# Moving the operands of one matmul family by 192 bytes: longer tiles of probabilities and of r in an attention and feed-forward kernel

## The chip, the cores and the metric

The kernel runs on one core of a Trainium2 chip. The metric is the device time of one execution in microseconds (us); the number that stands for a kernel is the median of several executions. A core has a matrix engine (TensorE: PE for its matmuls, PEld for the loads of its stationary operand), VectorE (DVE), ScalarE (ACT), GpSimd (POOL), and SyncE (SP), which here issues the DMAs. SBUF is the working memory, with 128 partitions; an address below is a byte address within a partition. PSUM is the memory that matmuls write.

## The reference

Windowed attention with block summaries, and behind it a feed-forward layer with a squared ReLU. Cut to what matters:

```python
k_sum = k.reshape(B, H, nb, 32, D).max(axis=3)         # B, H, S, D = 4, 8, 768, 64
v_sum = v.reshape(B, H, nb, 32, D).mean(axis=3)
scores_l = where(|i - j| < 16, q @ k.T / 8, -1e9)
scores_s = q @ k_sum.T / 8 + log(32)
a = softmax(concat([scores_l, scores_s]))
x = (a @ concat([v, v_sum])).reshape(3072, 512)        # heads side by side
h = x @ w_in                                           # 512 x 2048
g = s * maximum(h, 0)**2 + b
return g @ w_out                                       # 2048 x 512
```

## The kernel before

The 3072 tokens are worked in 12 chunks of 256 (`c`). A chunk has three parts on PE. The attention of its 8 heads (lines 274 to 417) ends in the attended values. The hidden layer, `hidden` (line 460), makes for each of 16 blocks of 128 hidden units (`f`) one 128x256 result in PSUM. The projection, `project` (line 504), adds each block's contribution to two 128x512 outputs.

Both matrix products of the feed-forward layer are done at fp32 accuracy with the one-pass type F32R, by splitting each operand into an upper and a lower part and adding three products: lower times upper, upper times lower, upper times upper. The attended values of a chunk are split into `xh` and `xl` (128 partitions, 4 blocks of 256 values, 4096 bytes a partition, two buffers each, so that one chunk's can be written while the other's are read). The weights are split into `wh` and `wl`. The activated values `g` are split into halves `gh` and `gl` (512 values, 2048 bytes, four buffers each).

The operand that is loaded into the array and stays there is the stationary one; the operand that is streamed past it is the moving one. In `hidden` the moving operand is a block of 256 values of `xh` or `xl`, and the stationary one 128 columns of `wl` or `wh`. In `project` it is the other way about: 512 columns of `wh` or `wl` move, and 128 columns of `gh` or `gl` are stationary. Every matmul of the two has its own load, so PE runs through pairs of a load and a matmul: 12 pairs for one `f` of `hidden`, 6 for one of `project`.

From chunk 2 on a planner sets the order: steps are numbered by hidden block; `hidden` is called for four blocks in a row (48 pairs), then `project` for the four blocks before (24 pairs). Beside these run the attention of a later chunk and the chain that makes `g`: `activate` (relu on ACT into `r`, square in place), `scaled` (POOL, in place), `upper_rows` (`gh`, DVE) and `lower_rows` (`gl`, DVE). The first chunks are written out by hand in `FIRST_ORDER`.

Where a tile lies is set by the pool it comes from. Pools stand one behind the other, and within a pool each name has its buffers one behind the other, in the order in which names are first asked for, each rounded up to 32 bytes. In the pool `p2` the order is `vsum`, `ksum`, `rs`, `pT`, `pr`, `mn`, `sums`, `xh`, `xl`, `r`, `gh`, `gl`, `vhalf`, `vmean`; behind it stands the pool with `qk` and `vw`. `pr` (probabilities of a pair of head pairs, made in `masked`) and `r` (made in `activate`) have two buffers each. In the weights' pools every tile is a multiple of 4096 bytes long, and all `wh` and `wl` start at a multiple of 256. Addresses before, with the remainder by 256:

| tile | first buffer | remainder of its buffers by 256 |
|---|---|---|
| wh (8 tiles), wl (16 tiles) | 4352 and 69888 on | 0 |
| pr | 163264 | 192, 224 |
| mn, sums | 171008, 171136 | 0 to 224 in steps of 32 |
| xh | 171264 | 0, 0 |
| xl | 179456 | 0, 0 |
| r | 187648 | 0, 0 |
| gh | 191744 | 0 in all four |
| gl | 199936 | 0 in all four |
| qk | 208896 | 0, 160, 64, 224 |
| vw | 220800 | 128 in all four |

Of the kernel before, what the change touches and what calls it, by code (L numbers as in the profile page):

```python
# [11 lines left out]
F32 = mybir.dt.float32  # L12
# [7 lines left out]
P = 128  # L20
# [7 lines left out]
KR = WIN + NB  # L28
NSUB = 4
T = NSUB * SUB  # L30
# [14 lines left out]
def windowed_attention_then_relu2_ffn(ctx, tc, qk, vwin, kt, vt, kq, vrow, wp, out):  # L45


    nc = tc.nc
# [5 lines left out]
    p2 = ctx.enter_context(tc.tile_pool(name="p2", bufs=2))  # L54
# [29 lines left out]
    def mask_of(st):  # L84
        return mask_first if st == 0 else mask_last if st == NST - 2 else mask_mid
# [143 lines left out]
    def place(c):  # L229
        return c // PER_B, c % PER_B  # L230
# [75 lines left out]
    def masked(c, p, j):  # L306
        _, ci = place(c)
        if j == 0 and c == 0:
            t = stage.tile([P, 4 * KR + 8], F32, name="pr0", tag="stage")
            pr_of[c, p] = t[:, : 4 * KR].rearrange("p (n k) -> p n k", k=KR)  # L310
            mn_of[c, p], sm_of[c, p] = t[:, 4 * KR : 4 * KR + 4], t[:, 4 * KR + 4 :]
        elif j == 0:
            if (c, p // 2) not in prs_of:
                prs_of[c, p // 2] = p2.tile([P, 8 * KR + 8], F32, name="pr", bufs=2)
                if turns_on_dve(c):
                    nc.gpsimd.memset(prs_of[c, p // 2][:, 8 * KR :], 0.0)
            t = prs_of[c, p // 2][:, 4 * KR * (p % 2) : 4 * KR * (p % 2 + 1)]
            pr_of[c, p] = t.rearrange("p (n k) -> p n k", k=KR)
            mn_of[c, p] = p2.tile([P, 4], F32, name="mn", bufs=4)
            sm_of[c, p] = p2.tile([P, 4], F32, name="sums", bufs=4)  # L320
        for e in range(2):
            n = 2 * e + j
            nc.vector.tensor_tensor_reduce(  # L323
                out=pr_of[c, p][:, n, :], in0=ps_of[c, p][e][:, j, :], in1=mask_of(NSUB * ci + 2 * j),
                scale=-1.0 / math.sqrt(D), scalar=3.0e38, op0=ALU.add, op1=ALU.min,
                accum_out=mn_of[c, p][:, n : n + 1],
            )
        if j == 1:
            ps_of.pop((c, p))
            qk_t.pop((c, p))  # L330
# [17 lines left out]
    prs_of, pTs_of = {}, {}  # L348

    def turns_on_dve(c):  # L350
        return c > 2
# [84 lines left out]
    ph_of, gg, po = {}, {}, {}  # L436
# [25 lines left out]
            )  # L462

    def activate(c, q, other=0):
        gg[c, q] = r = p2.tile([P, 2 * T], F32, name="r")
        ph = ph_of.pop((c, q))
        if other < 2:
            nc.scalar.activation(r, ph, AF.Relu)  # L468
        else:
            nc.vector.tensor_scalar(r, ph, 0.0, None, ALU.max)  # L470
        if other % 2:
            nc.vector.tensor_tensor(r, r, r, ALU.mult)
        else:
            nc.scalar.activation(r, r, AF.Square)  # L474
# [72 lines left out]
    def of(fn, *more):  # L547
# [4 lines left out]
        "i": of(load_weights, "in"), "o": of(load_weights, "out"), "w": of(load_weights, "in", "out"),  # L552
        "u": load_unit, "x": load_values, "L": load_k,
        "W": keep_warm, "K": k_max, "k": fill_k, "Z": scores_of_maxima, "S": scores, "M": masked, "E": exps,
        "N": normalize, "T": transposes, "C": turned, "V": values, "U": values_of_means, "R": mean_of_rows,
        "F": mean_done, "t": fill_v, "X": attended, "y": attended_low, 
        "Ai": of(scale_weights, "in"), "Ao": of(scale_weights, "out"), "A": of(scale_weights, "both"),
        "Bi": of(convert_weights, "in"), "Bo": of(convert_weights, "out"), "D": of(convert_weights, "both"),
        "Y": hidden_part, "H": hidden, "J": activate, "G": scaled, "a": upper_rows, "b": lower_rows,
        "P": project, "O": evict, "h": upper_weights, "l": lower_weights,  # L560
    }
# [20 lines left out]
    for c in range(2, NC):  # L582
        bi, ci = place(c)
        for p in range(NPAIR):
# [15 lines left out]
            for j in range(2):  # L600
                then(base, VISIT, scores, c, p, j)
                then(m, NEXT if p < 2 else ATT, masked, c, p, j)
                then((e0, e1)[j], NEXT if p < 2 else ATT, exps, c, p, j)
# [16 lines left out]
    for i in range(NF, NC * NF):  # L620
        c, f = divmod(i, NF)

        then(i - i % 4, HID, hidden, c, f)
        if f % 2:
            for stage_of in (activate, scaled, upper_rows, lower_rows):
                then(i, CHAIN, stage_of, c, f // 2)
        then((i + 4) | 3, PROJ, project, c, f)
        if f == NF - 1:
            for t in range(T // P):
                then((i + 4) | 3, EVICT, evict, c, t)  # L630
# [60 lines left out]
```

## Time and profile before

| | us |
|---|---|
| median of 3 runs (620.56 to 621.52) | 621.0 |
| the profiled execution's own time | 620.62 |
| its span, first to last instruction | 618.9 |
| granted TensorE clock in it | 0.999 |

The profile is of one execution. A view that groups instructions gives, for a line of the kernel, an engine and an operation, the count, the busy time and the mean or median duration of one. The durations of matmuls overlap, since one starts while the one before is still running out; how often PE starts a matmul is read from start times or from the pieces of the chain. The chain that ended last is followed back from the last instruction to whatever released it, and is PE for nearly its whole length.

### The profile page before, as it was taken

How to read it: one execution, taken by the hardware profiler on the slowest of the kernel's cores; microseconds unless marked ns; L12 is line 12 of the kernel's file. 1: busy time of each engine (PE TensorE's matmuls, PEld its weight loads, DVE VectorE, ACT ScalarE, POOL GpSimd, SP SyncE). 2: the span in 40 equal slices, each digit the busy share in tenths (PEclk: the TensorE clock that was granted, in tenths of full speed). 3: DMA queues.
4: the chain of work that ended last, by engine and by line, in shares of the span. 5: the costliest groups of instructions: out<-in, count | busy, mean ns of one | idle time of the engine just before them, and what ended most of it. 6: DMA issues, size and time to landing. Idle time of an engine off the chain costs nothing.

```text
span 618.9 us, 13522 instructions
## 1 busy us (share of the span) xinstructions
PE 608.4 (98%) x5240; PEld 551.3 (89%) x5240; DVE 418.7 (68%) x1126; ACT 276.6 (45%) x712; POOL 138.0 (22%) x275
## 2 busy tenths in 40 slices
PE   6999999999999999999999999999999999999997
PEld 5798999899889998998999899999998998999896
DVE  6999988689488278568758648947848827832211
ACT  5999997262352362263163154234235235223221
POOL 4420012211410411411131411321141051041110
PEclk9999999999999999999999999999999999999999
DMA  8998722026105017003503112500710500200000
GB/s 338 398 412 325 280 71 109 23 86 195 57 2 182 1 44 255 23 20 103 169 20 128 56 44 72 207 19 28 214 49 1 183 4 16 86 1 1 35 1 34
DMA packets 26993, 66.41 MB, mean 107 GB/s; under 512 B 3824, under 2 KB 3824, under 8 KB 26928
## 3 DMA queue, kind: packets, MB, share of 16 engines
q1 hardware_dynamic: 26928, 65.54, 29.9%
q8 instruction: 41, 0.67, 0.4%
q14 instruction: 24, 0.20, 0.1%
HBM read 59.09 MB, written 6.29 MB: 106 GB/s over the span
## 4 chain that ended last, share of the span: by engine, by line
PE 94%; ACT 3%; POOL 1%; DVE 1%; issue 1%; POOLq 0%; DVEq 0%; ACTq 0%
PE ph L460 44%; PE po L504 43%; PE pav L417 4%; PE ps L301 3%; ACT pr L336 2%; PE pt L379 0%; POOL vw L263 0%; PE ph L441 0%; DVE pr L346 0%; ACT pT L221 0%; ACT wraw L122 0%; ACT wraw L123 0%; POOL mask_first L73 0%; ACT vsum L221 0%; POOL mask_mid L73 0%
## 5 line engine op out<-in xcount | busy, mean ns | idle before, releaser
L481 POOL TENSOR_SCALAR r<-r,sb_col 128x512 f32<-128x512 f32 x85 | 68.9, 811 | 396.2 <-ACT r L474 281.2
L504 PE MATMUL po<-wh,gl 128*128 128x512 f32 x384 | 151.5, 395 | 0.0
L504 PE MATMUL po<-wl,gh 128*128 128x512 f32 x384 | 150.0, 391 | 0.0
L504 PE MATMUL po<-wh,gh 128*128 128x512 f32 x384 | 149.6, 389 | 0.0
L468 ACT ACTIVATE r<-ph 128x512 f32<-128x512 f32 x93 | 55.5, 597 | 209.9 <-PE ph L460 201.8
L219 DVE CAST gh<-r 128x512 fp32r<-128x512 f32 x88 | 38.3, 435 | 143.0 <-POOL r L481 140.3
L368 DVE STREAM_TRANSPOSE pT<-pr 32x256 f32<-32x256 f32 x288 | 125.5, 436 | 4.1
L460 PE MATMUL ph<-xl,wh 128*128 128x256 f32 x760 | 122.2, 283 | 0.0
L460 PE MATMUL ph<-xh,wh 128*128 128x256 f32 x760 | 122.1, 283 | 0.0
L460 PE MATMUL ph<-xh,wl 128*128 128x256 f32 x760 | 122.0, 283 | 0.0
L460 PEld LDWEIGHTS ph<-xh,wl 128*128 128x128 f32 x760 | 108.0, 191 | 4.3 <-issue 0.2
L460 PEld LDWEIGHTS ph<-xh,wh 128*128 128x128 f32 x760 | 104.9, 192 | 0.0
L460 PEld LDWEIGHTS ph<-xl,wh 128*128 128x128 f32 x760 | 104.8, 192 | 0.0
L504 PEld LDWEIGHTS po<-wh,gh 128*128 128x128 f32 x384 | 72.1, 188 | 15.5
L504 PEld LDWEIGHTS po<-wh,gl 128*128 128x128 f32 x384 | 72.3, 188 | 14.9 <-issue 1.0
L504 PEld LDWEIGHTS po<-wl,gh 128*128 128x128 f32 x384 | 72.3, 188 | 12.9
L336 ACT ACTIVATE pr<-pr,mn 128x120 f32<-128x120 f32 x176 | 67.0, 383 | 23.0 <-DVE mn L323 22.8
L492 DVE TENSOR_TENSOR gl<-r,gh 128x512 fp32r<-128x512 f32 x96 | 69.2, 721 | 4.1 <-ACT gh L221 1.3
L474 ACT ACTIVATE r<-r 128x512 f32<-128x512 f32 x92 | 58.1, 632 | 5.4 <-DVE r L470 2.5
L263 POOL COPY vw<-vsum 24x256 f32<-24x256 f32 x88 | 46.7, 565 | 37.1 <-DMA vsum<-vmean 16.4
L221 ACT COPY o<-po 128x512 f32<-128x512 f32 x23 | 13.5, 587 | 45.5 <-PE po L504 44.4
L346 DVE TENSOR_TENSOR pr<-pr,rs 128x480 f32<-128x480 f32 x48 | 32.1, 670 | 2.4 <-ACT pr L336 0.5
(88 smaller groups left out, 480.2 us busy)
## 6 DMA issues: line engine op xcount, KB each, us to landing
wraw<-in_wp_dram SPq DMA_DIRECT2D x32, 512.0 KB
qk<-in_qk_dram SPq DMA_DIRECT2D x44, 369.0 KB
vw<-in_vwin_dram SPq DMA_DIRECT2D x48, 256.0 KB
out_dram<-o SPq DMA_DIRECT2D x24, 256.0 KB
kraw<-in_kt_dram SPq DMA_DIRECT2D x12, 384.0 KB
vraw<-in_vt_dram SPq DMA_DIRECT2D x12, 252.0 KB
kq<-in_kq_dram SPq DMA_DIRECT2D x4, 512.0 KB
vraw<-in_vt_dram SPq DMA_DIRECT2D x6, 264.0 KB
```

Source lines behind the costliest of these rows:

```text
L219: nc.vector.tensor_copy(out_, in_)
L263: nc.gpsimd.tensor_copy(vw_t[c, p][WIN:KR, e], vsum[bi][WIN : WIN + NB, 2 * p + e, :].unsqueeze(1).to_broadcast([NB, NSUB, D]),)
L336: nc.scalar.activation(pr, pr, AF.Exp, bias=mn_of[c, p][:, n : n + 1], scale=-1.0, accum_out=sm_of[c, p][:, n : n + 1])
L346: nc.vector.tensor_tensor(pr, pr, rs.unsqueeze(2).to_broadcast([P, 4, KR]), ALU.mult)
L368: nc.vector.transpose(to[BLOCK * k : BLOCK * (k + 1), :, rows], src)
L417: nc.tensor.matmul(oi, vw[:KR, e, i, :], pi[:KR], start=True, stop=True)
L460: nc.tensor.matmul(ph, w[:, kc * P : (kc + 1) * P], x[:, kc], start=(n == 0), stop=(n == len(terms) - 1))
L468: nc.scalar.activation(r, ph, AF.Relu)
L474: nc.scalar.activation(r, r, AF.Square)
L481: (nc.vector if other else nc.gpsimd).tensor_scalar(g, g, s_col, b_col, ALU.mult, ALU.add)
L492: nc.vector.tensor_tensor(gl, g, gh.bitcast(F32), ALU.subtract)
L504: nc.tensor.matmul(po[c, t], a[:, t * P : (t + 1) * P], w[:, 512:], start=(f == 0 and n == 0), stop=(f == NF - 1 and n == len(terms) - 1),)
```

## The change

Two tiles are asked for at a greater length than is used. `pr` gets 24 more floats (96 bytes) in each of its two buffers, and only the 8 floats that were there are set to zero, as before. `r` gets 8 more floats (32 bytes) in each of its two buffers, and the code goes on with the first 512. No instruction is added, taken away, resized or put elsewhere in the order: on each engine the rows of the two programs are the same.

```diff
-                prs_of[c, p // 2] = p2.tile([P, 8 * KR + 8], F32, name="pr", bufs=2)
+                prs_of[c, p // 2] = p2.tile([P, 8 * KR + 32], F32, name="pr", bufs=2)
                 if turns_on_dve(c):
-                    nc.gpsimd.memset(prs_of[c, p // 2][:, 8 * KR :], 0.0)
+                    nc.gpsimd.memset(prs_of[c, p // 2][:, 8 * KR : 8 * KR + 8], 0.0)
...
-        gg[c, q] = r = p2.tile([P, 2 * T], F32, name="r")
+        gg[c, q] = r = p2.tile([P, 2 * T + 8], F32, name="r")[:, : 2 * T]
```

What moves is addresses. Everything behind `pr` in the pool moves up by 2 x 96 = 192 bytes, and everything behind `r` by 192 + 2 x 32 = 256:

| tile | moved by | remainder by 256 before | after |
|---|---|---|---|
| wh, wl, pT, first buffer of pr | 0 | 0, 0, 192, 192 | the same |
| second buffer of pr | 96 | 224 | 64 |
| mn, sums | 192 | 0 to 224 | 0 to 224 |
| xh, xl (moving operands of `hidden`) | 192 | 0 | 192 |
| r, first and second buffer | 192, 224 | 0, 0 | 192, 224 |
| gh, gl (stationary operands of `project`) | 256 | 0 | 0 |
| qk, vw | 256 | 0, 160, 64, 224 and 128 | the same |

So, by the remainder, the one relation between two operands of a matmul that changes in the feed-forward layer is that of `hidden`: the moving operand starts at 192 where its stationary one starts at 0, where both started at 0.

## The prediction

> **What bounds the kernel now.** I read the page's list of engines first, then the chain that ended last, by line.
>
> ```profile
> span 618.9 us, 13522 instructions
> PE 608.4 (98%) x5240; PEld 551.3 (89%) x5240; DVE 418.7 (68%) x1126; ACT 276.6 (45%) x712; POOL 138.0 (22%) x275
> PE 94%; ACT 3%; POOL 1%; DVE 1%; issue 1%; POOLq 0%; DVEq 0%; ACTq 0%
> ```
>
> PE is busy 98% of the span and the chain lies on it for 94%. A busy PE is not yet a PE at its peak, so the next question is how fast the pairs of load and matmul follow each other. The chain in order of time gives that, because it joins pairs of one line to a piece with a length and a count. Near the end:
>
> ```profile
> 569.92 0.84 PE ph L460 x7
> 570.76 5.47 PE po L504 x24
> 576.22 5.75 PE ph L460 x48
> 581.98 5.47 PE po L504 x24
> 587.44 5.75 PE ph L460 x48
> 593.20 5.47 PE po L504 x24
> 598.66 5.75 PE ph L460 x48
> 604.42 10.92 PE po L504 x48
> ```
>
> Columns: start, length, what, how many. Line 460 (`hidden`) takes 5.75 / 48 = 119.8 ns a pair and 0.84 / 7 = 120 ns within a run; line 504 (`project`) 5.47 / 24 = 227.9 ns. No wait is in between: a piece starts where the last one ended. The kernel's time is therefore mostly two pitches times two counts, and a change of addresses can move it only by moving a pitch, or by turning something beside PE into a wait.
>
> **How much of the pitch is not streaming.** The profile has a family of matmuls that shows what a pair can do, the transposes of line 379.
>
> ```profile
> 108.98 0.82 PE L379 MATMUL pt<-ident,pr 128*120 128x128 f32 x6
> L379 PE MATMUL pt<-ident,pr x48: 270/273/326, 12.6 to 109.7; 128*120 128x128 f32 x48
> ```
>
> Six of them take 0.82 us, the last one's 273 ns included: (820 - 273) / 5 = 109 ns from start to start. Now the two lines of the feed-forward layer, with the least, median and greatest duration of one:
>
> ```profile
> L460 PEld LDWEIGHTS ph<-xh,wl x760: 186/192/192, 36.3 to 603.1; 128*128 128x128 f32 x190
> L460 PE MATMUL ph<-xh,wl x760: 277/283/387, 36.4 to 603.2; 128*128 128x256 f32 x190
> L460 PE MATMUL ph<-xl,wh x760: 280/283/287, 36.9 to 603.7; 128*128 128x256 f32 x190
> L504 PE MATMUL po<-wl,gh x384: 387/389/402, 42.4 to 614.7; 128*128 128x512 f32 x192
> ```
>
> From 256 to 512 columns the median grows by 389 - 283 = 106 ns, so 256 columns stream in about 106 ns. A pair of line 460 thus has 120 - 106 = 14 ns beside its columns, one of line 504 has 227.9 - 212 = 16. But line 460 also has matmuls of 277 ns and loads of 186 where the medians are 283 and 192: something between them costs about 6 ns each, nearly always, and sometimes doesn't.
>
> Where doesn't it? At the switch from `project` to `hidden`. Matmuls from 597.82 us on, start, length and count:
>
> ```profile
> 597.82 0.39 PE L504 MATMUL po<-wh,gl 128*128 128x512 f32 x1
> 598.05 0.39 PE L504 MATMUL po<-wl,gh 128*128 128x512 f32 x1
> 598.27 0.39 PE L504 MATMUL po<-wh,gh 128*128 128x512 f32 x1
> 598.50 0.64 PE L460 MATMUL ph<-xh,wl 128*128 128x256 f32 x4
> 598.97 0.64 PE L460 MATMUL ph<-xl,wh 128*128 128x256 f32 x4
> 599.45 0.28 PE L460 MATMUL ph<-xh,wh 128*128 128x256 f32 x1
> ```
>
> The first four pairs of `hidden` take 0.47 us (598.50 to 598.97), the next four 0.48. The grouped view of the stretch 598.4 to 598.6 has the first alone:
>
> ```profile
> L460 PE MATMUL ph<-xh,wl 128*128 128x256 f32 x1 | 0.3, 278 | 0.0
> ```
>
> It lasts 278 ns, and the pitch behind it is 114 ns; by the third pair it is 120 and stays there. In the other direction the same happens. The first matmuls of `project` after `hidden`:
>
> ```profile
> 593.03 0.40 PE L504 MATMUL po<-wh,gl 128*128 128x512 f32 x1
> 593.27 0.40 PE L504 MATMUL po<-wl,gh 128*128 128x512 f32 x1
> 593.50 0.39 PE L504 MATMUL po<-wh,gh 128*128 128x512 f32 x1
> 593.73 0.40 PE L504 MATMUL po<-wh,gl 128*128 128x512 f32 x1
> 593.96 0.39 PE L504 MATMUL po<-wl,gh 128*128 128x512 f32 x1
> 594.19 0.39 PE L504 MATMUL po<-wh,gh 128*128 128x512 f32 x1
> 594.42 0.39 PE L504 MATMUL po<-wh,gl 128*128 128x512 f32 x1
> ...
> 597.82 0.39 PE L504 MATMUL po<-wh,gl 128*128 128x512 f32 x1
> ```
>
> Six pairs take 1.39 us, 232 ns each; the 15 from 594.42 to 597.82 take 3.40, 226.7 each. The same tiles at the same remainders by 256 run at 232 and at 226.7, and at 114 and at 120. So the pitch depends on how the load of the next pair stands in time to the matmul that is streaming, and each of the two lines settles into a state of its own. That is what two streams do that read one memory and now and then hold each other up. `hidden` has settled in a state with the 6 ns, `project` in one without.
>
> **The change part by part.** No instruction, wait, DMA or size changes, so there is nothing to add up but durations.
>
> *xh and xl at 192.* If the hold-up depends on where in a stretch of 256 bytes the two streams are, then moving one of them by 192 is like shifting it in time. The moving stream passes 1024 bytes in 106 ns, so 64 bytes (192 is 64 short of 256) are 6.6 ns, more than the few ns in which the pitch went from 114 to 120. The state that `hidden` settles in is then chosen anew. No row shows a full-rate pair at another remainder, so the price has to be bounded. Best seen: 114 ns, which is -6. Worst seen: the longest matmul within an undisturbed run is 287 ns against 283, which is +4. I take the middle between the best seen and what it is now, 117 ns, because the 277 ns are seen at starts of runs alone and never held there.
>
> Count: chunks 2 to 11 have 10 x 16 x 12 = 1920 pairs, all in stretches such as the one above; the first two chunks have another 384, laid among waits of the start, of which I count half. (1920 + 192) x 3 ns = 6.3 us. Bounds: (1920 + 384) x 6 = 13.8 us less, 2304 x 4 = 9.2 us more.
>
> The Trainium skill has a rule against the change having any effect. Its page "TensorE: Matmul & The Clock Gate", under "Step-by-step: what each phase is for", says that PE has two independent read ports in SBUF and that loading the next weights takes no bandwidth from the running matmul. By it the sum would be 0 in place of -6.3 us. The rows at the switches bear it out only in part, since 278 and 283 ns for equal matmuls need some cause.
>
> *What the gain must pass.* If `hidden` gets faster, the chain that makes g has less time. The rows of its five steps, with the least, median and greatest duration:
>
> ```profile
> L468 ACT ACTIVATE r<-ph x93: 576/598/655, 37.7 to 604.8; 128x512 f32<-128x512 f32 x93
> L481 POOL TENSOR_SCALAR r<-r,sb_col x85: 757/771/1262, 70.3 to 606.2; 128x512 f32<-128x512 f32 x85
> L474 ACT ACTIVATE r<-r x92: 622/632/637, 38.3 to 605.4; 128x512 f32<-128x512 f32 x92
> L219 DVE CAST gh<-r x88: 412/427/834, 40.1 to 607.0; 128x512 fp32r<-128x512 f32 x88
> L492 DVE TENSOR_TENSOR gl<-r,gh x96: 682/693/1064, 41.1 to 607.5; 128x512 fp32r<-128x512 f32 x96
> ```
>
> The medians, 598 + 632 + 771 + 427 + 693, add up to 3.1 us. Between the last of four blocks of `hidden` and its projection lie a group of 24 projection pairs and one of 48 hidden pairs, 11.2 us, and 48 x 6 ns = 0.3 us less leaves that far from a wait. So a gain on PE is kept.
>
> *r at 192 and 224, pr's second buffer at 64, mn and sums.* These are read and written by DVE, ACT and POOL.
>
> ```profile
> L368 DVE STREAM_TRANSPOSE pT<-pr x288: 425/436/442, 134.8 to 543.3; 32x256 f32<-32x256 f32 x144
> ```
>
> The transposes of `pr` read buffers at 192 and 224 by turns and all last 425 to 442 ns, so there the remainder shows no price; for `r` no row has another than 0. I cost them at nothing. What hides it is the 11.2 us for a chain of 3.1: even 25% more on each of the five steps is 0.8 us and reaches no wait. Without that cover it would be 0.8 us for each of the last few blocks, about 1 us.
>
> *gh, gl, qk, vw* move by 256 and keep their remainders. Only the entry into `project` could change, since `hidden` may leave PE in another state. Six pairs at 232 for 226.7 are 32 ns, and with 48 entries 1.5 us: that much less at best, and as much more for a longer settling. I take 0.
>
> **The sum.** 620.6 - 6.3 = 614.3 us against the profiled execution's own time (618.9 of span and 1.7 around it); the median of the runs shown, 621.0, is 0.4 above. I forecast 614.3 us.
>
> **The rivals.**
>
> *No effect (621 us).* The 14 ns beside the columns are a fixed price of such a pair, and the 6 ns come from timing alone, by the array's hand-over from one set of weights to the next. For it: the transposes of line 379 have their stationary operand at 192, 160, 128, 96, 64, 32, 0 and 224 in turn against a moving one at 128, and 273 ns and 109 ns throughout. Against it: these stream half as fast (128 columns in the time of 256), so each read has slack, and a hold-up needn't show. Also for it: each line settles by itself, and may settle at the same 120 again. It is also the time that the rule of the Trainium skill's page on TensorE, above, would give. Price 0, with an entry's 1.5 us to either side and the scatter of the runs: 619.4 to 622.2.
>
> *Slower (626 to 630 us).* The same mechanism with the other sign. At equal remainders the two streams may start in step and meet at the ends of the load, where it costs least; 64 bytes apart they may meet in its midst, at each pass. The price is the matmul of 287 ns, a pitch of 124: 2304 x 4 ns = 9.2 us, 629.8 us; half of that gives 625.2. It decides as soon as the settled matmul is over 283 ns; at 284 it is +2.3 us. For it speaks that `project`, also at equal remainders, has settled in its good state, so equal remainders aren't bad as such. Against it, that `hidden` has settled in a state that is already 5 to 6 ns over its best and only 4 under its worst.
>
> *Much faster (608 us).* `hidden` settles at 115 or below: -5 x 2304 = -11.5 us, 609.1, and 606.8 at 114. Only the first pair of a run shows it now.
>
> **How the numbers follow.** A measurement of this kernel tells about 0.2% (1.2 us) from no change. Faster by 1.2 to 9 us with the forecast at its middle: 0.34. Much faster: 0.09. No effect within 1.2 us: 0.31; its outer parts, a little over 1.2 to either side, are counted with faster and slower at 0.01 each. Slower: 0.24. Together faster 0.44, same 0.31, slower 0.25. The forecast's own range is 611.6 to 619.4. The range that should hold 8 in 10 has to reach over both signs: 608.5 leaves out about half of the much faster case, and 627.5 leaves out the worse half of the slower one, 0.05 and 0.12.
>
> **What would show it.** The durations of line 460's matmuls decide: a median of 280 or below, and pieces of 48 pairs at 5.6 us, and the forecast's step is right; 283 and 5.75 say no effect; 285 or more and pieces over 5.85 say slower. Line 504 should keep its 389 ns and its 5.47 us. POOL's 771, ACT's 632 and the casts should stay; if they don't and no wait of PE appears, that is the cover named above. The prediction is wrong if line 460's matmuls keep 283 while the pitch moves, since then the loads set it; or if line 504 moves, whose operands kept their remainders.

## The result, and the profile after

The changed kernel takes 615.07 us (median of 4 runs, 614.38 to 615.96) against 620.78 us for the kernel before on the same chips. The ratio is 0.9908, with a 95% interval of 0.9888 to 0.9928. The profiled execution's own time is 615.71 us.

The page of the profile after, span and engines:

```profile
span 614.0 us, 13522 instructions
PE 602.5 (98%) x5240; PEld 545.7 (89%) x5240; DVE 418.2 (68%) x1126; ACT 276.3 (45%) x712; POOL 138.8 (23%) x275
```

The span is 4.9 us shorter, and PE's busy time falls by 5.9 us while those of DVE, ACT and POOL stay within 0.8. The chain that ended last, in order of time, shows where (start, length, what, how many):

```profile
566.26 5.44 PE po L504 x24
571.70 5.65 PE ph L460 x48
577.35 5.44 PE po L504 x24
582.79 5.65 PE ph L460 x48
588.44 5.44 PE po L504 x24
593.88 5.65 PE ph L460 x48
599.54 10.89 PE po L504 x48
```

48 pairs of `hidden` take 5.65 us where they took 5.75, so 117.7 ns a pair for 119.8. 24 pairs of `project` take 5.44 for 5.47. Chunks 2 to 11 have 40 groups of each: 40 x 0.10 + 40 x 0.03 = 5.2 us, where the span fell by 4.9.

In the first two chunks two things cancel. Counted from start to start, their 360 pairs of line 460 take 1.2 us less than before. But at 39 to 42 us PE starts four pairs of this line late, 222 to 679 ns after the one before, and the waits of the first two chunks grow by 1.3 us. The view of waits after the change (in total, times, longest) has both the wait and what stands behind it:

```profile
PE ph L460 <- ACT r L468: 0.6, 2, 0.4
ACT wraw L122 <- DMA wraw<-in_wp_dram: 2.2, 2, 1.1
```

ACT came late to `activate`, since it had first waited 1.1 us for a DMA of weights and started the instruction behind it at 36.88 us, where before it started at 35.59. Before, PE has no wait for ACT in `hidden`. In two of the runs below, x192 and rel, where `hidden` has the same new difference, ACT starts that instruction at 35.66 and 35.70, so the new difference alone doesn't bring the late transfer.

Durations by line (least, median, greatest):

```profile
L460 PEld LDWEIGHTS ph<-xl,wh x760: 187/188/192, 36.8 to 598.7; 128*128 128x128 f32 x190
L460 PE MATMUL ph<-xh,wl x760: 276/281/386, 36.4 to 598.3; 128*128 128x256 f32 x190
L460 PE MATMUL ph<-xl,wh x760: 276/281/281, 36.9 to 598.8; 128*128 128x256 f32 x190
L504 PE MATMUL po<-wl,gh x384: 387/389/402, 43.4 to 609.8; 128*128 128x512 f32 x192
```

The median matmul of `hidden` went from 283 to 281 ns and the median load from 192 to 188, with no instruction changed. `project` keeps its 389. Its 0.03 us come from the entry. Its first matmuls after `hidden`, from the timeline:

```profile
588.28 0.39 PE L504 MATMUL po<-wh,gl 128*128 128x512 f32 x1
588.51 0.39 PE L504 MATMUL po<-wl,gh 128*128 128x512 f32 x1
588.73 0.39 PE L504 MATMUL po<-wh,gh 128*128 128x512 f32 x1
588.96 0.39 PE L504 MATMUL po<-wh,gl 128*128 128x512 f32 x1
589.19 0.39 PE L504 MATMUL po<-wl,gh 128*128 128x512 f32 x1
589.41 0.39 PE L504 MATMUL po<-wh,gh 128*128 128x512 f32 x1
```

Five pitches in 1.13 us are 226 ns each: the slow settling at 232 that stood here is gone. So `hidden`, whose own operands moved, also hands PE over in another state.

### The profile page after: what moved, and what is told of

Same layout as the page of the kernel before. It is cut to its first block, busy times and chain, and to the rows that moved or that the text cites. A ratio compares the mean times of both kernels' runs of the same rounds, so it can differ in the third digit from the quotient of the medians.

```text
span 614.0 us, 13522 instructions
## 1 busy us (share of the span) xinstructions
PE 602.5 (98%) x5240; PEld 545.7 (89%) x5240; DVE 418.2 (68%) x1126; ACT 276.3 (45%) x712; POOL 138.8 (23%) x275
## 4 chain that ended last, share of the span: by engine, by line
PE 88%; DVE 4%; ACT 3%; DMA 3%; issue 1%; SPq 1%; POOL 0%; POOLq 0%; ACTq 0%; DVEq 0%
PE po L504 40%; PE ph L460 39%; PE pav L417 3%; PE ps L301 3%; ACT pr L336 2%; DVE pT L368 2%; DMA wraw<-in_wp_dram 1%; DMA vsum<-vmean 1%; PE warm L199 1%; DVE pr L346 1%; DMA kq<-in_kq_dram 1%; PE pt L379 1%; SPq L180 0%; POOL vw L263 0%; DVE gl L492 0%
## 5 line engine op out<-in xcount | busy, mean ns | idle before, releaser
L460 PE MATMUL ph<-xl,wh 128*128 128x256 f32 x760 | 120.2, 281 | 0.0
L460 PE MATMUL ph<-xh,wh 128*128 128x256 f32 x760 | 120.2, 281 | 0.0
L460 PEld LDWEIGHTS ph<-xh,wl 128*128 128x128 f32 x760 | 106.2, 189 | 5.6 <-ACT r L468 1.2
L460 PEld LDWEIGHTS ph<-xh,wh 128*128 128x128 f32 x760 | 103.3, 190 | 0.0
L460 PEld LDWEIGHTS ph<-xl,wh 128*128 128x128 f32 x760 | 102.6, 189 | 0.0
```

Of the source, the lines that this page charges most:

```text
L460: nc.tensor.matmul(ph, w[:, kc * P : (kc + 1) * P], x[:, kc], start=(n == 0), stop=(n == len(terms) - 1))
```

## The experiments

The theory: a load that runs beside a streaming matmul disturbs it by an amount that depends on the difference of their addresses (taken by 256), and on the moment in which the load starts against the stream. The main rivals: one of the other moved tiles made the gain; or the moving operand's own address counts, and not a difference.

Each kernel is the one before with tiles of nothing (`pad_...`) laid ahead of others in the same pool, or a longer tile; on each engine the instructions stand in the order of before. Edits are shown against the kernel before. Pads of `pad_x` stand ahead of `xh`, `pad_r` ahead of `r`, `pad_g` ahead of `gh`, one buffer each, and are asked for once. The number in `[P, n]` is in floats.

### x192: xh and xl alone

```diff
-            xt[c] = p2.tile([P, NKC, T], F32R, name="xh", tag="xh")
+            xt[c] = (c == 0 and p2.tile([P, 48], F32, name="pad_x", bufs=1), p2.tile([P, NKC, T], F32R, name="xh", tag="xh"))[1]
...
-        gg[c, q] = r = p2.tile([P, 2 * T], F32, name="r")
+        gg[c, q] = r = ((c, q) == (0, 0) and p2.tile([P, 16], F32, name="pad_r", bufs=1), p2.tile([P, 2 * T], F32, name="r"))[1]
```

> Alone xh and xl are moved to 192 by 256 (192 bytes of nothing ahead of xh, 64 ahead of r); pr, mn, sums and r keep their remainders, gh and gl stay at 0. Theory 1 (two streams of a pair disturb each other by where they stand in 256 bytes): the whole gain is here, 615 us, line 460 at 281 ns a matmul and 5.65 us for 48 pairs. Rival (the other tiles that moved, r or pr, made it, or the start of the program settles differently by chance): 621 us and 283 ns.

615.58 us, ratio 0.9909 (0.9894 to 0.9924): the whole of the gain. The chain has the same two lengths as after the change:

```profile
571.54 5.65 PE ph L460 x48
577.20 5.44 PE po L504 x24
```

### r_only: r alone

```diff
-        gg[c, q] = r = p2.tile([P, 2 * T], F32, name="r")
+        gg[c, q] = r = ((c, q) == (0, 0) and p2.tile([P, 48], F32, name="pad_r", bufs=1), p2.tile([P, 2 * T + 8], F32, name="r"))[1][:, : 2 * T]
```

> Alone r is moved, to 192 and 224, by the same 32 bytes in each buffer; xh and xl stay at 0, gh and gl at 0. Theory 1: nothing happens, 621 us, line 460 at 283 ns and 5.75 us. Rival (r is written and read by ACT, POOL and DVE while PE streams, and its remainder decides who disturbs whom): 615 to 618 us, with POOL's 819 ns as after the change where it was 811.

621.08 us, ratio 1.0003 (0.9990 to 1.0016), and the chain has the lengths of before:

```profile
577.73 5.75 PE ph L460 x48
583.49 5.47 PE po L504 x24
```

Of the change's parts, the move of `r` does nothing, and with x192 the move of `pr`, `mn` and `sums` has nothing left to explain.

### rel: difference or address

All weights, `gh` and `gl` go to 64, and `xh` and `xl` stay at 0.

```diff
-    mean4 = const.tile([P, 2 * NB - 4], F32, name="mean4")
+    mean4 = const.tile([P, 2 * NB - 4 + 16], F32, name="mean4")[:, : 2 * NB - 4]
...
-            xt[c] = p2.tile([P, NKC, T], F32R, name="xh", tag="xh")
+            xt[c] = (c == 0 and p2.tile([P, 48], F32, name="pad_x", bufs=1), p2.tile([P, NKC, T], F32R, name="xh", tag="xh"))[1]
...
-        gh = p2.tile([P, 2 * T], F32R, name="gh", bufs=4)
+        gh = ((c, q) == (0, 0) and p2.tile([P, 16], F32, name="pad_g", bufs=1), p2.tile([P, 2 * T], F32R, name="gh", bufs=4))[1]
```

> xh and xl stay at 0, but all weights are moved to 64, and gh and gl to 64 with them. The moving operand of line 460 is then 64 short of its stationary one, as after the change, with another absolute remainder; in line 504 both are at 64, with no difference, as before. Theory 1 in its relative form: 615 us, 281 ns and 5.65 us in line 460, 389 ns in line 504. Rival, the absolute form (what counts is the moving operand's own remainder): 621 us and 283 ns, as xh and xl are at 0, and line 504 is the one that may move.

615.73 us, ratio 0.9914 (0.9893 to 0.9935).

```profile
570.61 5.65 PE ph L460 x48
576.26 5.44 PE po L504 x24
```

`xh` and `xl` lie where they did before, and the lengths are those of after. So it is the difference of the two operands that counts. The absolute form falls.

### g192: only the 96 bytes of pr

The change without the 32 bytes of `r`, so that `gh` and `gl` come to lie at 192.

> Only the 96 bytes of pr, without those of r: xh and xl at 192, and gh and gl at 192 as well, where they are stationary and the weights that move past them are at 0. Theory 1: line 460 keeps 281 ns and 5.65 us; line 504 has a new difference between its two streams and its pitch moves from 226.7 ns, which at 1152 pairs is 1.2 us for each ns; its state was the good one already, so I expect it no better, 389 to 393 ns, 615 to 620 us. Rival (only the moving operand's own remainder counts): line 504 keeps 389 ns and 5.44 us, and the time is 615 us.

610.80 us, ratio 0.9848 (0.9820 to 0.9877), the fastest of all. My expectation of 615 to 620 was wrong, and in an unexpected place. Chain and durations:

```profile
577.52 5.47 PE ph L460 x48
582.98 5.49 PE po L504 x24
```

```profile
L460 PE MATMUL ph<-xl,wh x760: 276/276/281, 36.9 to 593.2; 128*128 128x256 f32 x190
L504 PE MATMUL po<-wl,gh x384: 388/392/398, 42.4 to 604.3; 128*128 128x512 f32 x192
L504 PE MATMUL po<-wh,gh x384: 392/394/398, 42.6 to 604.5; 128*128 128x512 f32 x192
```

`project`, whose difference changed, gets a little slower, as the theory has it: 5.49 us for 5.44. But `hidden`, whose operands lie exactly as after the change, settles at 276 ns and 5.47 us, 113.9 ns a pair. The difference alone doesn't fix the pitch; there are two settled states at the same difference. The trace has the passage from the one to the other inside each group: on the mean of the groups of 48, the first three pairs run at 117 to 118 ns, as after the change, then come one of 123 and one of 118, and from the sixth on the pitch is 113 to 114. Against before, 40 x (0.28 - 0.02) = 10.4 us, and the span went from 618.9 to 608.5, by 10.4; so near a match is luck in part, since the first chunks and the attention moved as well.

### x0_g192: the new hand-over without the new difference

```diff
-        gh = p2.tile([P, 2 * T], F32R, name="gh", bufs=4)
+        gh = ((c, q) == (0, 0) and p2.tile([P, 48], F32, name="pad_g", bufs=1), p2.tile([P, 2 * T], F32R, name="gh", bufs=4))[1]
...
-        vs = p2.tile([96, D], F32, name="vmean", bufs=1)
+        vs = p2.tile([96, D + 16], F32, name="vmean", bufs=1)[:, :D]
```

> gh and gl at 192, all else at the remainders of before (xh and xl at 0, r at 0). In g192 line 504 went to 5.49 us for 24 pairs and line 460 from 5.65 to 5.47 for 48, though line 460's own operands lay as after the change. Theory 1 with memory (a line's settled state depends on its own difference and on the state in which the other line hands over): line 504 at 5.49 as in g192, and line 460 either held at 283 ns and 5.75 us by its own difference of 0, time about 622 us, or thrown by the new hand-over into the state with 277 ns, 5.5 us and 610 us. Rival (g at 192 makes line 460 fast by itself, whatever x): 276 ns, 610 us. The first is likelier, 622 us.

622.07 us, ratio 1.0019 (1.0010 to 1.0029).

```profile
588.88 5.75 PE ph L460 x48
594.63 5.49 PE po L504 x24
600.12 5.76 PE ph L460 x48
```

`project` costs its 5.49 again, and `hidden` stays at 5.75 to 5.76. So `gh` and `gl` at 192 don't do it without the difference of 64 short, and after, x192 and rel show that the difference doesn't do it without such a hand-over. A `project` with `gh` and `gl` at 192 is not the only one that hands over well: the next run reaches 5.46 with another. But in no run does a group of 48 get below 5.6 us at another difference than 64 short.

### x192_g64: two states in one run

`xh` and `xl` at 192, `gh` and `gl` at 64: x192 without `pad_r`, and with a `pad_g` of 32 floats.

> xh and xl at 192 as after the change, gh and gl at 64, so that in line 504 the moving weights stand 64 short of their stationary operand, the difference that line 460 has. Theory 1: line 504 gets a pitch of its own again, and hands over in another state; if 64 short is the good side for it too, it keeps 226.7 ns or less, and line 460 settles at 276 or 281 ns: 608 to 615 us. If its best was at 0: 390 to 394 ns, 5.5 us, 611 to 618 us. Remainders of qk and vw change as well (64 more), which at lines 301 and 417 I expect to show nothing.

618.02 us, ratio 0.9956 (0.9940 to 0.9971), at the upper end of what I had expected for the case that `project` loses, and `project` loses more than the 5.5 us that I had put there. The chain, with the attention of two chunks left out:

```profile
467.17 5.66 PE ph L460 x48
472.82 5.60 PE po L504 x24
478.42 5.46 PE ph L460 x48
483.88 5.59 PE po L504 x24
489.47 5.66 PE ph L460 x48
495.13 5.60 PE po L504 x24
500.73 5.46 PE ph L460 x48
...
562.62 5.46 PE ph L460 x48
568.08 5.59 PE po L504 x24
573.67 5.66 PE ph L460 x48
579.33 5.60 PE po L504 x24
584.93 5.46 PE ph L460 x48
```

`hidden` takes 5.66 and 5.46 us by turns. The groups that start at 467.17 and 562.62 are the first of chunks that are two apart, with the same weights and the same buffers of `xh`, `xl`, `gh` and `gl`; one takes 5.66 and the other 5.46. So nothing in the addresses tells them apart, and the state in which PE comes to them must. The trace bears that out. Within a chunk the group of `project` ahead of one of 5.46 takes 5.60 us, and that ahead of one of 5.66 takes 5.59. By start times, the last pair of `project` lasts 235 or 236 ns ahead of each of the 20 groups of 5.46 and 229 or 230 ahead of each of the 19 groups of 5.66, without exception among the 39 groups of chunks 2 to 11 that follow 24 pairs of `project`. It is a sign of the state and no rule by itself, as 230 and 231 ns stand ahead of the 5.47 us of g192. `project` at this difference is the dearer one, 5.59 to 5.60.

### x64, x128, x224: other differences

As x192, with pads ahead of `xh` of 16, 32 and 56 floats and ahead of `r` of 48, 32 and 8, so that `gh` and `gl` stay at 0.

> xh and xl at 64, the moving operand 64 ahead of the stationary one; r, gh and gl at 0. If any distance from 0 helps: 281 ns and 615 us. If the sign matters, as in line 504 of g192, whose moving operand was 64 ahead and which got 1 to 2 ns a pair slower: 283 ns or more and 621 to 625 us. I think the second likelier, by little.

> xh and xl at 128, half of 256 away; r, gh and gl at 0. If what counts is where in 256 bytes the faster stream passes the slower one, the passes lie elsewhere than at 0 and 192, and 276 to 281 ns are as likely as 283: 612 to 621 us. If only a multiple of 128 counts (or 64 with its sign), 283 ns and 621 us.

> xh and xl at 224, 32 short of the weights; r, gh and gl at 0. This asks in what steps the remainder counts. If the steps are 64 bytes, 224 lies in the same 64 bytes as 192 and line 460 settles at 281 ns, 615 us; if they are finer, it is a case of its own, between 113 and 121 ns a pair, 607 to 622 us.

x64: 617.19 us, ratio 0.9947 (0.9933 to 0.9962). x128: 621.77 us, 1.0016 (1.0006 to 1.0025). x224: 618.03 us, 0.9960 (0.9946 to 0.9974). Their chains, in this order:

```profile
578.53 5.48 PE po L504 x24
584.01 5.66 PE ph L460 x48
```

```profile
582.60 5.48 PE po L504 x24
588.08 5.76 PE ph L460 x48
```

```profile
578.83 5.49 PE po L504 x24
584.31 5.68 PE ph L460 x48
```

64 ahead helps `hidden` nearly as much as 64 short; I had thought the other case likelier. 128 does not help, and 32 short is a case of its own, so the steps are not 64 bytes. For `hidden`, 0 and 128 come out alike, and so do 64 and 192: its pieces alone would fit a step of 128 as well as one of 256, and no run moves its operands by 256 against each other. `project` keeps its operands in all three and still goes from 5.44 (x192) to 5.48 and 5.49: that is the hand-over the other way.

### x192_g224, g192q and gh192_gl0: where the best lies

x192_g224 has `gh` and `gl` at 224: x192 without `pad_r`, with a `pad_g` of 8 floats. g192q has x192's `pad_x`, no `pad_r`, and x0_g192's longer `vs`, so that `xh`, `xl`, `gh` and `gl` are at 192 and `pr`, `qk` and `vw` as before. gh192_gl0 has x192's `pad_x`, no `pad_r`, and 16 floats ahead of `gl`.

> xh and xl at 192, gh and gl at 224, so in line 504 the moving weights are 32 ahead of the stationary operand (64 ahead in g192, 0 after the change). Theory 1 with memory: the hand-over to line 460 is a new one; if it falls into the 276 ns state as in g192 and line 504 costs 5.44 to 5.49 us, 608 to 611 us; if line 460 falls into its 281 ns state, 615 us or a little over.

> xh, xl, gh and gl at 192 as in g192, while pr, qk and vw keep the remainders of before. If the gain of g192 comes from the two lines of the feed-forward layer (theory 1 with memory): again 611 us, 276 ns and 5.47 us in line 460, 5.49 us in line 504. If the other remainders of qk and vw or of pr's second buffer made the hand-overs what they were: between 611 and 616 us.

> As g192q, but gl at 0, so that two of three loads of line 504 are at 192 and one at 0. The aim is the 276 ns state of line 460 with less than the 5.49 us of line 504. The hand-over to line 460 comes from a pair with gh. If gl's pairs go back to their 226.7 ns and the hand-over stays that of g192: 5.47 and about 5.46 us, 609 to 610 us. If the hand-over changes: line 460 at 281 ns and 5.65 us, 615 us or more.

x192_g224 is a miss: 620.52 us, ratio 0.9997 (0.9988 to 1.0007). In 31 of the 39 groups `hidden` has the gain of after, and in 8 it takes 5.45 us, again two states at the same addresses. `project` gives the gain back:

```profile
581.33 5.60 PE po L504 x24
586.93 5.66 PE ph L460 x48
```

g192q: 611.46 us, ratio 0.9858 (0.9841 to 0.9875), an interval that overlaps that of g192, and the same lengths in 35 of the 39 groups:

```profile
578.97 5.47 PE ph L460 x48
584.44 5.49 PE po L504 x24
```

In the other four `hidden` takes 5.65 to 5.66 us, and there the last pair of `project` lasts 226 or 227 ns, where it lasts 231 or 236 ahead of the 35. Those four cost about 0.8 us, the size of the step from 610.80 to 611.46. So the remainders of `pr`, `qk` and `vw` aren't what made g192. gh192_gl0: 617.31 us, ratio 0.9954 (0.9940 to 0.9969):

```profile
584.19 5.65 PE ph L460 x48
589.85 5.49 PE po L504 x24
```

With `gl` alone at 0, `project` stays at 5.49 and `hidden` falls back into its 5.65 state. Nothing was won, and the hand-over turns on `gl` too.

All of it in one table. "Ahead" is the moving operand's remainder less the stationary one's, by 256, with 192 written as -64.

| kernel | ahead in hidden | ahead in project | 48 of hidden, us | 24 of project, us | ratio |
|---|---|---|---|---|---|
| before, r_only | 0 | 0 | 5.75 | 5.47 | 1, 1.0003 |
| after, x192, rel | -64 | 0 | 5.65 | 5.44 | 0.9908, 0.9909, 0.9914 |
| g192, g192q | -64 | 64 | 5.47 (in 4 of 39 groups of g192q 5.65) | 5.49 | 0.9848, 0.9858 |
| x192_g64 | -64 | -64 | 5.46 (20 of 39 groups) and 5.66 | 5.59 to 5.60 | 0.9956 |
| x192_g224 | -64 | 32 | 5.66 and 5.45 (8 of 39 groups) | 5.60 | 0.9997 |
| gh192_gl0 | -64 | 64 for gh, 0 for gl | 5.65 | 5.49 | 0.9954 |
| x0_g192 | 0 | 64 | 5.75 | 5.49 | 1.0019 |
| x64 | 64 | 0 | 5.66 | 5.48 | 0.9947 |
| x128 | 128 | 0 | 5.76 | 5.48 | 1.0016 |
| x224 | -32 | 0 | 5.68 | 5.49 | 0.9960 |

## Why the prediction was right, and where it wasn't

The forecast of 614.3 us against the profiled execution's own time stands beside 615.71 measured, or beside a median of 615.07.

**The mechanism** was the step that everything hung on: that the surplus over the columns is partly two streams disturbing each other, that it depends on 256-byte remainders, and that `hidden` had settled in a bad state. x192, r_only and rel show that the pitch depends on the difference of the two operands' addresses; the settled median load of 188 for 192 ns and matmul of 281 for 283 show that `hidden` had a better state to go to. The 256 is shown in part: r_only moves `gh` and `gl` by 256 and `project` keeps its 5.47 us, but for `hidden` no run tells 256 from 128. That the two streams meet in the memory itself, rather than elsewhere on their way into the array, was argued and no run shows it.

**The pitch** was forecast at 117 ns, as the middle between the best seen and the present one, and came out at 117.7. Being so near was luck in part: the middle was a choice between two bounds, and no row gave it. At the same difference `hidden` also settles at 113.9 (g192), which I had held for a state of the first pair alone; the forecast's "never held there" was true of the profile before and not of the other runs.

**The count and the sum.** 2112 pairs at 3 ns gave 6.3 us. Measured from start to start, the 1920 pairs of chunks 2 to 11 take 4.15 us less and the 360 early ones of line 460 take 1.2 us less: 5.3 us, or 2.3 ns a pair, where I had 3. The early pairs gained in full, twice the 0.6 us that I had counted for half of them. The entries of `project` gave 1.2 us, where I had taken 0 and bounded it at 1.5. And in the profiled execution the early wait of 1.3 us, which the sum doesn't have, took back what the early pairs had won. Three sizes were off, and they partly cancelled; that the sum came out near is luck to that extent.

**What was costed at nothing** was nothing: r_only shows it for `r`, and the five steps of the chain that makes g keep their medians to 1 ns.

**The signs to look for** were too narrow. I asked for a median of 280 or below and pieces of 5.6 us; 281 and 5.65 came. And I wrote that line 504 would keep 5.47 us and that the prediction would be wrong if it moved. It moved by its entry, through the hand-over that I had named and set to 0.

**The rivals.** "No effect" falls with the intervals of after, x192 and rel: with the same instructions, a pair of `hidden` takes 113.9 to 120 ns by where the tiles lie. With it falls the 0 that the prediction drew from the rule of the Trainium skill's page "TensorE: Matmul & The Clock Gate", section "Step-by-step: what each phase is for", by which loading the next weights takes no SBUF read bandwidth from the running matmul. Whether the bandwidth is what the two streams contend for, no run here shows. "Slower" did not happen at -64, but its mechanism is there: at 128 (x128) `hidden` gains nothing and the kernel is 0.16% slower, and `project` loses 0.13 us a group at -64 and 32. "Much faster" happened in g192. That is the version that beats both kernels: the change without the 32 bytes of `r`, at 610.8 us.

## What to carry to other kernels

Where PE is bound by pairs of a load and a matmul, compare the pitch from start to start with the time of the columns alone, and look at the first pairs after a switch of operands: if equal pairs run at two pitches, the addresses of the two operands are a knob worth a few runs. Pad both operands in turn, since it is their difference that counts, and judge by the whole stretch and by all its groups, since a pad on one product changes the state in which it hands over to the next, and equal groups can settle in two states. A good remainder for one pair of operands is no rule for another: -64 was good in `hidden` and bad in `project`.

## What the hardware showed that I had not expected

PE keeps its rhythm across a change of operands: in x192_g64 groups with the same instructions and the same addresses take 5.46 and 5.66 us by turns, 3.6% apart, for the length of 48 pairs, and the last pair before the switch (235 to 236 or 229 to 230 ns) tells which. The remainder counts in steps finer than 64 bytes, as 224 differs from 192 (5.68 against 5.65 us in `hidden`, and 5.49 against 5.44 in `project` through its entry). Why a difference of 64 either way is good in `hidden`, and why 0 is best for `project`, stays open; no run here looked inside a pair.
